# Three reorderings around the V half of a gated decode-attention kernel: idle products and denominators ahead of V's first unit, the last diagonal ahead of a scaling, and w2's extra rows behind O's turning

## The chip, the cores and the metric

The kernel runs on one core of one Trainium2 chip. The metric is the device time of one launch in microseconds. TensorE (PE) does the matrix products, VectorE (DVE) elementwise work, reductions and 32x32 transposes, ScalarE (ACT) exponentials and copies, GpSimd (POOL) builds constants and masks, and SyncE (SP) issues the transfers from device memory. Each engine runs its own list in order; they meet through semaphores.

## What is computed

```python
g = sigmoid((x * gate_w).sum(-1, keepdims=True))
q = x @ wq                      # 2 batches, 32 heads, head size 128, one token
scores = q . k_cache * 128**-0.5   # k_cache, v_cache: (2, 32, 4096, 128) bf16
o = softmax(scores) . v_cache
a = o.reshape(2, 1, 4096) @ wo  # wo: (4096, 512)
b = relu(B_x @ w1) @ w2         # w1: (512, 1376), w2: (1376, 512)
out = g * a + (1 - g) * b
```

One token per batch reads the whole K and V caches, 67 MB each, so there is about one multiply for each byte. (The reference feeds `A_x` to both branches.)

## The kernel before, in words

K and V stream through one SBUF buffer, `kv`, of five regions of 4 MB (A, Ah, B, Bh, C). A K piece is 4 or 8 MB, a V piece ("unit") 8 MB: the eight V units V0 to V7 go by turns into A+Ah (even units) and B+Bh (odd units). SP issues all transfers from one list in order (L339 to L353): the K pieces, the V units, two small transfers of w2's first 96 rows (`w2x`), `wo` in two parts (24 and 8 of its 32 row groups, into region C), and the remaining 1280 rows of w2 in three (`w2b`, `w2c`, `w2d`: 7, 2 and 1 row groups, into Ah). Each waits until the earlier holder of its region has been read: V2 for the last product of V0 (marker `v_read_0`), V3 for that of V1, and so on; the three parts of w2 wait for `v_read_6`.

In the K stage VectorE transposes each quarter of a piece (L483) and TensorE multiplies it with masked queries into four PSUM banks. `softmax` (L527) takes the maximum, lets ScalarE write four exponentials with their sums (`act_exp0` to `act_exp3`), and spreads the weights for V's first unit in two halves (`v_spread`, L552).

In the V stage each unit is 64 products of 32 weights by 512 columns, in four column groups of the array (L582). The unit's sums lie in bank 4 (even) or 5 (odd). `v_loop` is a hardware loop of four rounds, each an even unit, then a run of idle products, then an odd unit. An idle product multiplies constants into a bank that nobody reads; after each even unit there are 1 + `IDLE_ROUNDS` x `IDLE_EACH` = 55 of them. VectorE then takes the "diagonal" of the unit's bank (`v_extract`: a masked multiply, L602, and a reduction, L607).

The end of the kernel is a chain across engines: TensorE gathers the diagonals into O with a selection matrix (`o_gather`), VectorE scales O by the gate and by the reciprocal of the denominators (`o_scale`, once per batch), TensorE turns O into columns (`o_turn`) and VectorE copies them into `oW`. Then `project` multiplies w2's extra rows (indices -4 to -1) and the 32 row groups of `wo`, four at a time, into one bank; VectorE copies that bank (`pr_copy`), and `last_rows` sums it and adds the ten row groups of w2 left (L663, L670, L678). Two copies and one transfer store the 2 KB of output. The order of this end is written out by hand in the last lines of the kernel function; more idle products stand in it (`idle(4)`, `idle(8)`, `idle(4)`). The denominators (`o_denominators`) are two small products on TensorE and two reciprocals on VectorE.

Of the kernel before, what the change touches and what calls it, by code (L numbers as in the profile page):

```python
# [4 lines left out]
ALU = mybir.AluOpType  # L5
ACT = mybir.ActivationFunctionType
AX = mybir.AxisListType
# [10 lines left out]
WO_CUT = 24  # L18
WO_ALL = 32
WIDE = 5  # L20
IDLE_ROUNDS, IDLE_EACH = 6, 9


class _Marker:
# [106 lines left out]
def bass_gated_mix__gqa_block_cached__dense_activation_relu__decode_kernel(  # L131
# [19 lines left out]
    ident16 = sb("ident16", [128, 128], dt.bfloat16)  # L151
# [19 lines left out]
    qbuf = sb("qbuf", [128, 2, 2, 4, 160], dt.bfloat16)  # L171
# [15 lines left out]
    lsum = sb("lsum", [128, 2, 2], dt.float32)  # L187
    sel2 = sb("sel2", [128, WIDE], dt.float32)
    lrow = sb("lrow", [128, 2], dt.float32)
# [18 lines left out]
    def psf(p0, p1, c0, n):  # L208
        return PSF[p0:p1, c0:c0 + n]

    BANK = 512
    V_BANK = (4, 5)
# [11 lines left out]
    IDLE_C0 = 3 * BANK  # L224
# [50 lines left out]
    def dve(fn, waits=(), signal=None, dwaits=()):  # L275
        P.add("dve", fn, waits=[marker(w) for w in waits], signal=marker(signal) if signal else None, dwaits=dwaits)
# [4 lines left out]
    def pe(fn, waits=(), signal=None, dwaits=()):  # L281
        P.add("pe", fn, waits=[marker(w) for w in waits], signal=marker(signal) if signal else None, dwaits=dwaits)
# [5 lines left out]
         waits=["c_i16z"], signal="c_i16")  # L288
# [11 lines left out]
         waits=["c_s1"], signal="c_s2")  # L300
    pool(lambda g: g.affine_select(out=sell_odd, in_=sell_odd, pattern=[[4, 8], [32, 4]],
                                   compare_op=ALU.is_ge, fill=0.0, base=3, channel_multiplier=-1),
         waits=["c_s2"], signal="c_sell")
# [3 lines left out]
         waits=["c_m1"], signal="c_m2")  # L307
# [219 lines left out]
    def softmax():  # L527
        dve(lambda v: v.tensor_reduce(out=mpad[:, 0:2], in_=psf(0, 128, 0, 4 * BANK).rearrange("p (par n) -> p par n", par=2),  # L528
                                      axis=AX.X, op=ALU.max),
            waits=["pe_sc_end", "c_mpad"], signal="dve_m")  # L530
        dve(lambda v: v.transpose(out=mrow[:, :], in_=mpad[:, :]), waits=["dve_m"], signal="dve_mt")
        dve(lambda v: v.tensor_reduce(out=mmax[:], in_=mrow[:, :].rearrange("p (u c) -> p u c", c=4), axis=AX.X, op=ALU.max),
            waits=["dve_mt"], signal="dve_mm")
        dve(lambda v: v.tensor_scalar(out=nrow[:], in0=mmax[:].unsqueeze(2).to_broadcast([128, 8, 4]), scalar1=-INV_SQRT_DH,
                                      scalar2=None, op0=ALU.mult), waits=["dve_mm"], signal="dve_mn")
        dve(lambda v: v.transpose(out=negm[:, :], in_=nrow[:].rearrange("p u c -> p (u c)")),  # L536
            waits=["dve_mn"], signal="dve_neg")
        for g in range(2):
            for par in range(2):
                act(lambda a, g=g, par=par: a.activation(  # L540
                    out=E_sb[:, 32 * g:32 * g + 32, 16 * par:16 * par + 16], in_=psf(0, 128, (2 * par + g) * BANK, 512).rearrange("p (r s) -> p r s", s=16), func=ACT.Exp,
                    bias=negm[:, par:par + 1], scale=INV_SQRT_DH, accum_out=lsum[:, par, g:g + 1]),
                    waits=["dve_neg"], signal=f"act_exp{2 * g + par}")
            dve(lambda v, g=g: v.transpose(out=kt_late[:, 2048 + 1024 * g:3072 + 1024 * g].rearrange("p (r w) -> p r w", w=32), in_=E_sb[:, 32 * g:32 * g + 32, :]),  # L544
                waits=[f"act_exp{2 * g + 1}"], signal=f"dve_et{g}")
            v_spread(0, slice(32 * g, 32 * g + 32))
        dve(lambda v: v.tensor_reduce(out=lrow[:], in_=lsum[:], axis=AX.X, op=ALU.add), waits=["act_exp3"], signal="dve_lrow")  # L547

    def v_weights(n):
        return ptm[:, 2048 * (n % 2):2048 * (n % 2) + 2048].rearrange("p (n h c) -> p n h c", h=8, c=4)  # L550
# [1 line left out]
    def v_spread(n, rows=slice(0, 64), waits=()):  # L552
        shape = [128, rows.stop - rows.start, 8, 4]

        def fn(v):
            ins = v.tensor_tensor(out=v_weights(n)[:, rows], in0=ET_sb[:, rows, 4 * n:4 * n + 4].unsqueeze(2).to_broadcast(shape),  # L556
                                  in1=mask8[:].unsqueeze(1).unsqueeze(3).to_broadcast(shape), op=ALU.mult)
            return ins.then_inc(sem_pt[n % 2], 1) if rows.stop == 64 else ins
        dve(fn, waits=["dve_et1" if rows.stop == 64 else "dve_et0", "c_mask8"] + ([f"v_read_{n - 2}"] if n >= 2 else []))
# [2 lines left out]
        u, halves, region = v_pieces[n]  # L562
        return piece_sb(halves, region).rearrange("p (c n d) -> p c n d", c=4, d=128)

    def idle(n):
        out, lhsT, rhs = psf(0, 32, IDLE_C0, 512), ident16[:, 0:32], qbuf[:, :, :, :, 0:32]
        for j in range(n):
            if j:
                pe(lambda e: mm_held(e, out, lhsT, rhs, True, True, (128, 32), (0, 0)))
            else:  # L570
                pe(lambda e: e.matmul(out, lhsT=lhsT, rhs=rhs, start=True, stop=True, tile_position=(0, 0)))

    def v_loop():
        loop = _Loop(len(v_pieces) // 2)
        P.ops["pe"].append(loop)
        for x in range(2):
            rows = v_moving(x)
            for j in range(64):
                t = j % 4

                def fn(e, j=j, t=t, rows=rows, x=x):
                    ins = e.matmul(psf(32 * t, 32 * t + 32, V_BANK[x] * BANK, 512), lhsT=v_weights(x)[:, j], rhs=rows[:, :, j, :],  # L582
                                   start=(j < 4), stop=(j >= 60), tile_position=(0, 32 * t))
                    take = {0: (sem_pt[x], -1), 1: (sem_v[x], -16), 2: (sem_rd[1 - x], -1), 62: (sem_rd[x], 1)}.get(j)
                    return ins.then_inc(*take) if take else ins
                waits = [(sem_rd[1 - x], 1), (sem_pt[x], 1), (sem_v[x], 16)] if j == 0 else []
                marks = [marker(f"v_read_{2 * m + x}") for m in range(loop.n)] if j == 63 else None
                loop.ops.append(_Step(fn, waits, marks))
            if x == 0:
                out, lhsT, rhs = psf(0, 32, IDLE_C0, 512), ident16[:, 0:32], qbuf[:, :, :, :, 0:32]  # L590
                loop.ops.append(_Step(lambda e: e.matmul(out, lhsT=lhsT, rhs=rhs, start=True, stop=True, tile_position=(0, 0)), [], None))
                inner = _Loop(IDLE_ROUNDS)
                for j in range(IDLE_EACH):
                    inner.ops.append(_Step(lambda e: mm_held(e, out, lhsT, rhs, True, True, (128, 32), (0, 0)), [], None))
                loop.ops.append(inner)
# [14 lines left out]
    def o_denominators():  # L610
        for par in range(2):
            pe(lambda e, par=par: e.matmul(psf(0, 64, L_C0, 1), lhsT=sell[:, 1 - par:65 - par], rhs=lrow[:, par:par + 1],  # L612
                                           start=(par == 0), stop=(par == 1)),
               waits=["dve_lrow", "c_sell", "dve_h2"], signal=("pe_l" if par else None))
        for b in range(2):
            dve(lambda v, b=b: v.reciprocal(out=rinv[:, b:b + 1], in_=psf(32 * b, 32 * b + 32, L_C0, 1)), waits=["pe_l"],
                signal=("dve_rinv" if b else None))

    def o_gather(b, part):
        mine = range(n_first) if b == 0 else range(n_first, len(v_pieces))  # L620
        for n in part:
            w0 = 24 - 8 * (v_pieces[n][0] - 4 * b)
            pe(lambda e, n=n, w0=w0: e.matmul(psf(0, 32, O_C0[b], 128), lhsT=selx[:, w0:w0 + 32], rhs=X2[:, b, n - mine[0], :],  # L623
                                              start=(n == mine[0]), stop=(n == mine[-1])),
               waits=[f"dve_x{n}"] + (["dve_rinv", "dve_selx"] if n == mine[0] else []),
               signal=(f"pe_O{b}" if n == mine[-1] else None))

    def o_scale(b):
        dve(lambda v, b=b: v.tensor_scalar(out=O_sb[:, b, :], in0=psf(0, 32, O_C0[b], 128), scalar1=rinv[:, b:b + 1],  # L629
                                           scalar2=gb[0:32, b:b + 1], op0=ALU.mult, op1=ALU.mult),  # L630
            waits=[f"pe_O{b}", "dve_rinv", "dve_g"], signal=f"dve_O{b}")
# [22 lines left out]
    def pr_copy():  # L654
        dve(lambda v: v.tensor_copy(out=pr_sb, in_=psf(0, 128, PR_C0, 512)), waits=["pe_pr"], signal="dve_pr")
# [48 lines left out]
    softmax()  # L704
    last = len(v_pieces) - 1
    v_spread(1)
    o_denominators()
    v_loop()
    pr_clear()
    for n in range(last):  # L710
# [2 lines left out]
            v_spread(n + 2)  # L713
    o_gather(0, range(n_first))
    o_gather(1, range(n_first, last))
    o_scale(0)
    v_extract(last)
    project(range(-4, 0))
    idle(4)
    o_gather(1, (last,))  # L720
    o_scale(1)
    o_turn()
    idle(8)
    project(range(WO_ALL))
    idle(4)
    pr_copy()
    last_rows()
    store()
# [32 lines left out]
```

## Time and profile before

| what | value |
|---|---|
| time, median of 3 runs (lowest to highest) | 345.71 us (345.55 to 346.44) |
| the profiled execution's own time | 347.16 us |
| its span, first to last instruction | 345.9 us |
| mean granted TensorE clock | 0.887 of full |
| read from device memory | 145.43 MB, 420 GB/s over the span |
| share of the 16 DMA engines in the bulk queue | 97.6% |
| busy: TensorE / VectorE / ScalarE / GpSimd | 241.8 / 186.8 / 9.9 / 14.2 us |

The chain of waits is read from the last instruction back: each line is a start, a length and what ran. "DMA" in it is the time from a transfer's issue to its landing, so it includes waiting behind earlier transfers in the queue. The windows view gives for a stretch of time its length, the busy time of each engine with the count of instructions, the granted TensorE clock (1.00 or 0.50), the DMA share and the rate. A DMA packet of the caches is 64 KB and takes an engine about 2.42 us, and the 16 engines work nearly in step, so in windows of half a microsecond the rate comes in bursts.

### The profile page before, as it was taken

How to read it: one execution, taken by the hardware profiler on the slowest of the kernel's cores; microseconds unless marked ns; L12 is line 12 of the kernel's file. 1: busy time of each engine (PE TensorE's matmuls, PEld its weight loads, DVE VectorE, ACT ScalarE, POOL GpSimd, SP SyncE). 2: the span in 40 equal slices, each digit the busy share in tenths (PEclk: the TensorE clock that was granted, in tenths of full speed). 3: DMA queues.
4: the chain of work that ended last, by engine and by line, in shares of the span. 5: the costliest groups of instructions: out<-in, count | busy, mean ns of one | idle time of the engine just before them, and what ended most of it. 6: DMA issues, size and time to landing. Idle time of an engine off the chain costs nothing.

```text
span 345.9 us, 2803 instructions
## 1 busy us (share of the span) xinstructions
PE 241.8 (70%) x1446; PEld 51.8 (15%) x937; DVE 186.8 (54%) x122; ACT 9.9 (3%) x29; POOL 14.2 (4%) x41
## 2 busy tenths in 40 slices
PE   0467349799789799599899269819940697029797
PEld 0011001111111111011111020202020202011043
DVE  0229079899698999598998574134040040401021
ACT  1050000000000000000000300000000000000000
POOL 6000000000000000000000200000000000000000
PEclk9998959999989999879999859967985699759989
DMA  8998999999899998989999899989899998989892
GB/s 345 424 485 364 485 402 447 424 424 485 364 485 390 442 489 379 470 379 436 451 440 477 379 470 371 464 387 470 387 470 402 455 462 387 470 387 470 383 417 108
DMA packets 3648, 145.49 MB, mean 421 GB/s; under 512 B 413, under 2 KB 548, under 8 KB 828
## 3 DMA queue, kind: packets, MB, share of 16 engines
q1 hardware_dynamic: 3638, 145.43, 97.6%
q8 instruction: 3, 0.05, 0.1%
q10 hardware_dynamic: 6, 0.00, 0.0%
q14 instruction: 1, 0.01, 0.0%
HBM read 145.43 MB, written 0.00 MB: 420 GB/s over the span
## 4 chain that ended last, share of the span: by engine, by line
DMA 60%; DVE 20%; PE 17%; issue 2%; ACT 0%; SPq 0%; DVEq 0%
DMA kv<-in_A_k_cache_dram 32%; DMA kv<-in_A_v_cache_dram 28%; DVE kt L483 17%; PE PS L582 6%; PE PS L489 6%; PE PS L510 2%; DVE kt L556 1%; DVE kt L544 1%; DVE mpad L528 1%; PE PS L650 1%; PE PS L663 0%; ACT kt L540 0%; PE PS L623 0%; DVE kt L607 0%; PE PS L523 0%
## 5 line engine op out<-in xcount | busy, mean ns | idle before, releaser
L483 DVE STREAM_TRANSPOSE kt<-kv 128x2048 f32<-128x2048 f32 x64 | 141.2, 2274 | 25.6 <-DMA kv<-in_A_k_cache_dram 25.6
L510 PE MATMUL PS<-kt,qbuf 128*128 128x512 bf16 x256 | 106.5, 416 | 31.0 <-issue 22.6
L489 PE MATMUL PS<-kt,qbuf 128*128 128x512 bf16 x256 | 106.5, 416 | 0.0
L582 PE MATMUL PS<-kv,kt 128*32 128x512 bf16 x512 | 39.5, 468 | 45.5 <-DMA kv<-in_A_v_cache_dram 45.5
L602 DVE TENSOR_TENSOR kt<-PS,maskc 128x512 f32<-128x512 f32 x8 | 5.5, 688 | 85.6 <-PE PS L582 85.6
L489 PE MATMUL PS<-qbuf,ident 128*32 128x512 bf16 x229 | 50.6, 379 | 0.0
L510 PEld LDWEIGHTS PS<-kt,qbuf 128*128 128x128 bf16 x256 | 25.8, 101 | 140.6 <-issue 140.6
L582 PEld LDWEIGHTS PS<-kv,kt 128*32 128x32 bf16 x512 | 17.1, 114 | 113.0 <-issue 106.0
L556 DVE TENSOR_TENSOR kt<-kt,mask 128x2048 bf16<-128x2048 bf16 (+1 forms) x9 | 18.4, 2046 | 0.1
L407 POOL TENSOR_TENSOR qbuf<-qs,mask 128x64 bf16<-128x64 bf16 x16 | 6.5, 406 | 160.9 <-PE PS L489 141.1
L629 DVE TENSOR_SCALAR O_sb<-PS,rinv,gb 32x128 bf16<-32x128 f32 x2 | 0.8, 398 | 19.2 <-PE PS L623 19.2
L412 PE MATMUL PS<-kv,xTw 128*32 128x320 bf16 (+1 forms) x32 | 5.3, 692 | 5.2 <-DMA kv<-in_A_wq_dram 3.2
L607 DVE TENSOR_REDUCE kt<-kt 128x128 f32<-128x512 f32 x8 | 8.2, 1025 | 0.3
L540 ACT ACTIVATE kt<-PS,negm 128x512 bf16<-128x512 f32 x4 | 2.7, 686 | 168.9 <-DVE negm L536 168.9
L612 PE MATMUL PS<-lrow,sell 128*64 128x1 f32 x4 | 0.6, 250 | 9.8 <-DVE lrow L547 9.8
L436 DVE CAST qrow<-PS 128x256 bf16<-128x256 f32 x2 | 2.6, 1490 | 5.7 <-PE PS L489 5.7
L359 PE MATMUL PS<-ident,x_sb 3*128 3x3 bf16 x4 | 0.3, 167 | 6.7 <-DMA x_sb<-in_gate_w_dram 6.7
L693 ACT ACTIVATE out_sb<-PS 4x128 bf16<-4x128 f32 x1 | 0.3, 268 | 145.9 <-PE PS L678 145.9
L528 DVE TENSOR_REDUCE mpad<-PS 128x2 f32<-128x2048 f32 x1 | 2.3, 2292 | 3.1 <-PE PS L523 3.1
L362 DVE COPY xT<-PS 128x12 bf16<-128x12 bf16 x1 | 0.2, 169 | 7.0 <-PE PS L359 7.0
L489 PE MATMUL PS<-kv,xTw 128*32 128x512 bf16 (+1 forms) x24 | 3.7, 511 | 0.0
L544 DVE STREAM_TRANSPOSE kt<-kt 128x1024 bf16<-128x1024 bf16 x2 | 2.5, 1240 | 1.5 <-ACT kt L540 1.5
(84 smaller groups left out, 47.4 us busy)
## 6 DMA issues: line engine op xcount, KB each, us to landing
kv<-in_A_k_cache_dram SPq DMA_DIRECT2D x4, 4096.0 KB, 30.7
kv<-in_A_wq_dram SPq DMA_DIRECT2D x1, 4096.0 KB, 15.0
kv<-in_A_wo_dram SPq DMA_DIRECT2D x1, 3072.0 KB, 40.1
kv<-in_B_w_dram SPq DMA_DIRECT2D x1, 1376.0 KB, 5.9
kv<-in_A_wo_dram SPq DMA_DIRECT2D x1, 1024.0 KB, 42.2
kv<-in_B_w_dram SPq DMA_DIRECT2D x1, 896.0 KB, 26.1
kv<-in_B_w_dram SPq DMA_DIRECT2D x1, 256.0 KB, 26.4
kv<-in_A_v_cache_dram SPq DMA_DIRECT2D x8, 30.4
```

What stands on the lines that cost most here:

```text
L407: pool(lambda g: g.tensor_tensor(out=out, in0=src, in1=mask, op=ALU.mult).then_inc(sem_q[k % 2], 1), waits=waits)
L412: return e.matmul(out, lhsT=xTw[:, t, :], rhs=rhs, start=(t == 0), stop=(t == 3), tile_position=(0, 32 * c))
L483: dve(lambda v: v.transpose(out=dst, in_=pairs[:, h, 64 * a:64 * a + 64, :]).then_inc(sem_kt[i % SPAN], 1), waits=([f"pe_sc_{i - NKT}"] if ...
L489: return e.add_instruction(mybir.InstMatmult(start_tensor_calc=start, stop_tensor_calc=stop, tile_size=size, tile_position=at, ldweights=F ...
L510: ins = e.matmul(out, lhsT=lhsT, rhs=rhs, start=False, stop=False)
L528: dve(lambda v: v.tensor_reduce(out=mpad[:, 0:2], in_=psf(0, 128, 0, 4 * BANK).rearrange("p (par n) -> p par n", par=2), axis=AX.X, op=ALU ...
L544: dve(lambda v, g=g: v.transpose(out=kt_late[:, 2048 + 1024 * g:3072 + 1024 * g].rearrange("p (r w) -> p r w", w=32), in_=E_sb[:, 32 * g:3 ...
L556: ins = v.tensor_tensor(out=v_weights(n)[:, rows], in0=ET_sb[:, rows, 4 * n:4 * n + 4].unsqueeze(2).to_broadcast(shape), in1=mask8[:].unsq ...
L582: ins = e.matmul(psf(32 * t, 32 * t + 32, V_BANK[x] * BANK, 512), lhsT=v_weights(x)[:, j], rhs=rows[:, :, j, :], start=(j < 4), stop=(j >= ...
L602: dve(lambda e: e.tensor_tensor(out=parts[p0:p1], in0=psf(p0, p1, bank * BANK, 512).rearrange("p (c d) -> p c d", c=4), in1=maskc[p0:p1].u ...
L607: dve(lambda e: e.tensor_reduce(out=X2[:, b, k, :], in_=parts.rearrange("p c d -> p d c"), axis=AX.X, op=ALU.add), waits=[f"dve_m{n}"], si ...
L650: pe(lambda e, t=t, r=r, lhsT=lhsT, rhs=rhs: e.matmul(psf(32 * t, 32 * t + 2, PR_C0, 512), lhsT=lhsT, rhs=rhs, start=(r < 0), stop=(r >= W ...
```

## The change

Four edits. (1) `IDLE_ROUNDS` goes from 6 to 7: 64 idle products after each even unit in place of 55. (2) Before `v_loop`, 9 idle products that wait for the first exponential now stand ahead of the denominators and 5 more behind them, in the bank of the odd units; the sum of the exponentials' sums (`lrow`) moves on VectorE from behind the second half of the spread to behind the first. (3) On VectorE the diagonal of V7 goes ahead of the scaling of O's first batch. (4) On TensorE w2's extra rows move from ahead of the last gather to behind O's turning; the 4 idle products there and the 8 behind the turning go; 4 stand between the 24th and the 25th row group of `wo`, and 3 instead of 4 behind the last one. SP's list of transfers is the same.

```diff
-IDLE_ROUNDS, IDLE_EACH = 6, 9
+IDLE_ROUNDS, IDLE_EACH = 7, 9
...
             v_spread(0, slice(32 * g, 32 * g + 32))
-        dve(lambda v: v.tensor_reduce(out=lrow[:], in_=lsum[:], axis=AX.X, op=ALU.add), waits=["act_exp3"], signal="dve_lrow")
+            if g == 0:
+                dve(lambda v: v.tensor_reduce(out=lrow[:], in_=lsum[:], axis=AX.X, op=ALU.add), waits=["act_exp3"], signal="dve_lrow")
...
-    def idle(n):
-        out, lhsT, rhs = psf(0, 32, IDLE_C0, 512), ident16[:, 0:32], qbuf[:, :, :, :, 0:32]
+    def idle(n, at=IDLE_C0, after=None):
+        out, lhsT, rhs = psf(0, 32, at, 512), ident16[:, 0:32], qbuf[:, :, :, :, 0:32]
...
-                pe(lambda e: e.matmul(out, lhsT=lhsT, rhs=rhs, start=True, stop=True, tile_position=(0, 0)))
+                pe(lambda e: e.matmul(out, lhsT=lhsT, rhs=rhs, start=True, stop=True, tile_position=(0, 0)), waits=[after] if after else [])
...
     v_spread(1)
+    idle(9, V_BANK[1] * BANK, "act_exp0")
     o_denominators()
+    idle(5, V_BANK[1] * BANK)
     v_loop()
...
     o_gather(1, range(n_first, last))
+    v_extract(last)
     o_scale(0)
-    v_extract(last)
-    project(range(-4, 0))
-    idle(4)
     o_gather(1, (last,))
     o_scale(1)
     o_turn()
-    idle(8)
-    project(range(WO_ALL))
+    project(range(-4, WO_CUT))
     idle(4)
+    project(range(WO_CUT, WO_ALL))
+    idle(3)
     pr_copy()
```

## The prediction

> **What bounds the kernel now.** I read the chain of waits first, then the issues, then windows where the chain crosses the change. In the chain, each line is start, length, what ran.
>
> ```profile
> 133.08 29.76 DMA kv<-in_A_k_cache_dram
> ...
> 223.59 27.59 DMA kv<-in_A_v_cache_dram
> ...
> 293.72 34.88 DMA kv<-in_A_v_cache_dram
> 328.60 0.14 issue
> 328.74 5.32 PE PS L582 x64
> 334.06 0.86 PE PS L623 x8
> ...
> 335.35 0.61 DVE kt L602
> ...
> 335.98 1.03 DVE kt L607
> ...
> 338.24 0.32 PE PS L571
> ...
> 342.66 1.56 PE PS L663 x44
> ```
>
> Transfers carry everything up to V7's landing at 293.72 + 34.88 = 328.60; the rest is a tail of 17 us. V3 lands at 223.59 + 27.59 = 251.18, V5 at 289.88 (255.02 + 34.86 in the same chain), so 8 MB take 19.36 us when the queue is full. The K piece of the first line lands at 162.84; from there to V3's landing lie 4 MB of K and four V units, 4.5 x 19.36 = 87.1 us, but 88.34 pass: 1.2 us are lost. The same sum between the K landings at 113.10 and 162.84 (20 MB, 48.4 us, 49.74 taken) loses 1.3 too, so not every loss is a starved queue. Half-microsecond windows (length, busy times of PE, PEld, DVE, ACT, POOL, clock, DMA share, GB/s) show where V's loss is:
>
> ```profile
> 206.50:207.00 0.50, 0.50 (x16) 0.26 (x12) 0.00 (x0) 0.00 (x0) 0.00 (x0) 1.00 3.94 1704
> ...
> 209.00:209.50 0.50, 0.50 (x4) 0.00 (x0) 0.50 (x1) 0.00 (x0) 0.00 (x0) 1.00 2.43 787
> 209.50:210.00 0.50, 0.50 (x4) 0.00 (x0) 0.50 (x2) 0.00 (x0) 0.00 (x0) 1.00 1.11 393
> 210.00:210.50 0.50, 0.50 (x4) 0.00 (x0) 0.50 (x2) 0.00 (x0) 0.00 (x0) 1.00 2.07 786
> ...
> 212.50:213.00 0.50, 0.50 (x5) 0.00 (x0) 0.00 (x0) 0.00 (x0) 0.00 (x0) 1.00 2.72 1180
> ```
>
> Bursts come 2.42 us apart: 206.8, 209.2 and then 211.7 expected. The one at 209 is smeared to 210.5 with a larger share per byte (longer packets), and the next comes at 212.6, about 0.85 late. V2 was issued at 208.27, when V0's last product was read, and V1's transfer ran dry at 209.2. Why V0 was late, and what V7 paid, is in the timeline and in windows:
>
> ```profile
> 202.75 5.44 PE L582 MATMUL PS<-kv,kt 128*32 128x512 bf16 x64
> ...
> 251.32 3.64 PE L582 MATMUL PS<-kv,kt 128*32 128x512 bf16 x64 [1.31 <-DMA kv<-in_A_v_cache_dram]
> ...
> 328.74 5.32 PE L582 MATMUL PS<-kv,kt 128*32 128x512 bf16 x64 [2.47 <-DMA kv<-in_A_v_cache_dram]
> ```
>
> ```profile
> 325.92:329.33 3.41, 0.94 (x14) 0.39 (x16) 0.00 (x0) 0.00 (x0) 0.00 (x0) 1.00 0.96 411
> 329.33:332.74 3.41, 3.41 (x39) 1.57 (x32) 0.00 (x0) 0.00 (x0) 0.00 (x0) 0.50 1.05 454
> ```
>
> The same 64 products take 3.64 at full clock and 5.3 to 5.4 where half of it is granted. V3 (gap 1.31) stayed fast; V7, 2.47 behind the last idle product, met a half-clock stretch of 3.41 us. The end of the queue matters as much:
>
> ```profile
> kv<-in_A_wo_dram SPq DMA_DIRECT2D x1, 1024.0 KB, 42.2
> kv<-in_B_w_dram SPq DMA_DIRECT2D x1, 896.0 KB, 26.1
> kv<-in_B_w_dram SPq DMA_DIRECT2D x1, 128.0 KB, 26.2
> ```
>
> `wo`'s second part, issued at 296.24, lands at 338.4; `w2b`, issued at 314.5, at 340.6; `w2d`, issued at 315.3, at 341.5. TensorE ends at 344.35, so the tail is 2.4 us longer than the transfers allow.
>
> **The change, part by part.** Sums are against the profiled execution, 347.16 us: 1.26 around its span.
>
> *Start of V.* The first exponential is read out at about 196.45. Nine idle products cost 0.427 each at half clock, 0.216 at full (11.82 us for 55 behind V6); they end between 198.4 and 200.3. The `lrow` sum (0.15) comes earlier, at 199.8, so the denominators (0.58) end by 200.9, five more products by 202.0, or 203.0 if all at half clock. V0's weights are ready at 202.2 (0.1 later than before, `lrow` being ahead). So V0 starts at 202.2 to 203.0 against 202.82 and, TensorE having been busy through a 3.4 us stretch, takes 3.7: `v_read_0` at 205.9 to 206.7 against 208.2. V2 is issued at least 1.5 us earlier. Smeared packets began to arrive within 1 to 2 us of the issue at 208.27, so an issue before 207 closes the hole. Value: at most the whole loss, 1.25 (slowest engine, by landings), 0.85 by the bursts, and 0 if the slowest engine's loss has another cause, as the K stage's has. I take 1.05, between the two rows that measure this hole. If V0's cover went (V1's transfer), each microsecond of a later `v_read_0` would cost one.
>
> *64 idle products.* Nine more cost 1.94 us after V0, V2, V4, V6. V1 is waiting then already, but V0 ends 2.3 earlier, so V3 is issued about where it was (223.6), with V2 moving until 229. V3 and V5 start up to 0.7 late; their readers release V5 and V7, which queue 15 us behind other units: nothing. Behind V6 the idle products end at 327.7 (V6 starting 1.05 earlier at half clock, so ending 0.5 earlier) where V7 lands at 327.55 plus 0.14: no gap is left, and V7 takes 3.69 instead of 5.32: 1.63. If V6 runs wholly at half clock (V2 took 6.19), the idle run ends 0.6 later, a price of 0.6 on V7.
>
> *Diagonal ahead of scaling.* Before, VectorE waited for seven gathers (0.86 behind V7's end) and then scaled (0.40) ahead of the diagonal. Now the diagonal (0.61 + 1.03) starts as V7 ends; gathers run beside it; the scaling runs beside the last gather (0.42): 1.29 saved, 0 added.
>
> *The order of the projections.* Turning done, 8 idle products were 1.73 on TensorE's path, of which the copy to `oW` (0.34 and its signals) hid about 0.45: 1.25 saved. The four extra rows (0.22 to 0.4) now run beside that copy. Four idle products between the 24th and 25th row group (0.86) wait in the time in which `wo`'s second part lands; three at the end run beside `pr_copy` (0.69).
>
> Own work of the tail would thus end 1.63 + 1.29 + 1.25 = 4.2 earlier by itself, less up to 0.9 for the inserted idle products: 3.3. It can't all be had: `w2d` lands at 341.5, its products start 0.14 later (as V7's did) and the last ones take 0.3: 341.94 instead of 344.35, so 2.41. With the hole closed all landings come 1.05 earlier, and so does the end (by then the own work is ready: V7 ends at 331.4, `oW` at 334.8, `wo`'s rows done at 338.0, the sums ready at 339.1, `w2b` at 339.55). Sum: 347.16 - 2.41 - 1.05 = **343.7 us**.
>
> The runs shown have a median 1.45 below the profiled execution. Half clock in V7 costs 1.63, so I read this as most runs not paying it (347.16 - 1.63 = 345.53; the lowest is 345.55). The new end hangs on transfers, so 343.7 stands for the runs; if the 1.45 belongs to profiling, it is 342.3.
>
> One page speaks to this. The Trainium skill, "TensorE: Matmul & The Clock Gate", Part 1, says that the clock is granted by a free-running window of 3413 ns; the trace agrees (329.33 to 332.74, 3.41). By that rule the phase differs from run to run, V7's loss is in some runs only, and the gain against the median is about 2.0 rather than 3.5.
>
> **The rivals.** *The hole stays.* V2 waits for something else, or the slowest engine lost its time elsewhere (for: the equal loss in the K stage; against: bursts late just behind V2's issue). Then only the tail is saved: 347.16 - 2.41 = 344.75. The Trainium skill, "DMA: Bandwidth & Descriptors", Specifications, gives about 0.6 us to the first byte for SyncE's transfers; by it V2 could begin at 208.9, before the queue ran dry, and this rival would hold. The smeared packets at 209 to 210.5 speak against it.
>
> *The end goes to half clock.* TensorE now waits in pieces: behind the gathers, around the turning, for `w2b`. The leanest 3.41 us hold about 1.8 busy. In the profile 1.77 busy (288.37 to 291.78) kept full clock, 0.94 lost it. If it is lost, 44 products of 1.56 us take about 1.3 more behind `w2b`, of which 0.2 is hidden: 344.8.
>
> *Slower.* An idle run that overruns: 64 products behind V6 at half clock for two stretches of 3.41 us end 3.4 later, V7 starts at 331.1, and own work (3.69 + 7.7 + 1.4 from V7's start to TensorE's end) ends at 343.9: 346.7. It decides from 2.5 us of overrun. Against it: all four idle runs before were at clock 1.00 throughout.
>
> **How the numbers follow.** Forecast 0.66, with a range of its own of 342.3 to 344.4; hole stays 0.16; half clock at the end 0.12; overrun 0.06. The range of 8 in 10 is 342.3 to 344.9: from the offset case below to both rivals near 344.8. A difference of 0.3%, 1.04 us, is about what can be told from none: 344.67 and 346.75 are the edges. Faster: the forecast and some of the two rivals beside the edge, 0.8; within: most of those two, 0.15; slower: most of the overrun, 0.05.
>
> **What would show it.** V0 starts near 202.3, at 3.6 to 3.8, and SP issues V2 before 207; the bursts keep 2.42 us; V3 lands at 250.2 or less. V7 follows the idle products within 0.3 and takes 3.7. The masked multiply starts with V7's last product. TensorE waits for `w2b` and then `w2d`, and ends within 0.5 of `w2d`'s landing, near 340.9. Wrong would be: V2 issued earlier but landing at 231.8; clock 0.50 behind V7; an idle run that ends over 1 us behind V7's landing.

## The result, and the profile after

The changed kernel takes 343.82 us (median of 10 runs, 343.48 to 345.64), the kernel before in the same runs 346.32 (345.08 to 349.24): a ratio of 0.9933, 95% interval 0.9904 to 0.9961, so 2.3 us less by the ratio and 2.5 by the medians. The forecast was 343.7. The profiled execution of the changed kernel, at 345.64 us, is the slowest of the ten; a second trace of the same kernel (experiment 1) has 343.43. Both are read here, since the difference between them turned out to tell as much as the one between the kernels.

The chain of waits of the changed kernel, first trace (start, length, what):

```profile
202.74 4.46 PE PS L583 x48
207.20 0.02 issue
207.22 25.53 DMA kv<-in_A_v_cache_dram
232.75 0.14 issue
...
315.69 25.78 DMA kv<-in_B_w_dram
341.47 0.04 issue
341.52 1.17 PE PS L664 x36
...
342.84 0.28 DVE out_sb L693
```

The same of the second trace:

```profile
202.27 3.69 PE PS L583 x64
205.96 0.02 issue
205.97 24.49 DMA kv<-in_A_v_cache_dram
230.46 0.14 issue
...
313.63 25.65 DMA kv<-in_B_w_dram
339.27 0.04 issue
339.32 1.17 PE PS L664 x36
```

The end of the chain is no longer V7, gathers, diagonal, scaling and projections. It is the landing of `w2b`, the first and largest of w2's last three parts, and behind it 36 products. The prediction, too, had w2's transfers as the bound, but by way of the last part, `w2d`. The timeline shows the new order of the tail (second trace: start, busy time, engine, line, operation; in brackets the idle time before and what ended it):

```profile
327.36 3.64 PE L583 MATMUL PS<-kv,kt 128*32 128x512 bf16 x64
330.81 1.69 PE L624 MATMUL PS<-kt,selx 128*32 128x128 f32 x14
331.07 0.69 DVE L603 TENSOR_TENSOR kt<-PS,maskc 128x512 f32<-128x512 f32 x1 [15.68 <-PE PS L583]
331.79 1.03 DVE L608 TENSOR_REDUCE kt<-kt 128x128 f32<-128x512 f32 x1
...
334.72 1.47 PE L651 MATMUL PS<-kv,oW 128*2 128x512 bf16 x24 [0.34 <-DMA kv<-in_A_wo_dram]
...
339.32 1.17 PE L664 MATMUL PS<-kv,hT 128*4 128x128 bf16 x36 [0.19 <-DMA kv<-in_B_w_dram]
340.32 0.22 PE L489 MATMUL PS<-kv,hT 128*32 128x128 bf16 x2
```

The diagonal starts as V7's last product ends, beside the gathers. TensorE waits for `wo` and then for `w2b`. The last line shown is the first product of `w2d`'s row: it follows the 36 without a wait. V7 takes 3.64, right behind the idle products. From V7's landing to TensorE's last product 13.27 and 13.38 us pass in the two traces, 15.73 before; by the prediction's sum it was to be 13.34.

What differs between the two traces is the front. V0 took 4.62 in the first and 3.64 in the second, and V2 was issued at 207.22 and 205.97. The table has this for all traces of the study; landings are read from the signals that each of the 16 DMA engines gives for its share, so that the typical engine (median) can be told from the slowest, for which every reader has to wait. "End" is the end of TensorE's last product, and "w2" in the last column is the landing of `w2d`. V0's time runs from its first product to its last; in experiment 8 idle products run among V0's, so that it takes 4.69 there at full clock.

```
trace                     V0 takes  V2 issued  V2 lands: typical, slowest  V7 lands  end behind V7  end behind w2
before                        5.44     208.27     229.91    231.83           328.60       15.73          2.79
changed, first                4.62     207.22     229.09    232.75           329.53       13.27          0.33
1  changed, second            3.64     205.97     229.12    230.46           327.22       13.38          0.38
9  changed, third             3.64     205.91     229.03    230.56           327.32       13.38          0.35
2  start alone                3.64     206.04     228.99    230.50           327.25       14.04          1.09
3  64 idle products alone     6.15     208.92     230.46    233.36           330.55       14.75          1.83
4  both edits of the tail     6.22     208.77     230.26    231.86           328.64       13.30          0.34
5  changed, old start         6.55     209.22     230.75    232.38           329.16       13.30          0.36
6  changed, 55 products       3.79     206.21     229.12    230.83           327.58       14.24          1.28
7  a quarter of w2            3.64     206.18     229.19    231.04           327.82       13.04          2.20
8  V0 held back               4.69     209.41     230.94    232.56           329.34       13.31          0.38
10 warm start                 3.64     206.09     229.17    230.57           327.32       13.30          0.34
11 diagonal alone             5.58     208.25     229.87    232.48           329.25       13.44          0.52
12 projections alone          5.27     207.89     230.22    232.61           329.44       13.66          0.75
```

In the changed kernel's second trace V7 lands 1.38 us earlier than in the trace before (the prediction: 1.05), and the tail behind it is 2.35 shorter (2.41).

### The profile page after: what moved, and what is told of

The parts are those of the page before. It is cut to its first block, busy times and chain, and to the rows that moved or that the text cites. A ratio compares the mean times of both kernels' runs of the same rounds, so it can differ in the third digit from the quotient of the medians.

```text
span 344.4 us, 2854 instructions
## 1 busy us (share of the span) xinstructions
PE 251.2 (73%) x1487; PEld 52.1 (15%) x938; DVE 187.0 (54%) x122; ACT 9.9 (3%) x29; POOL 14.2 (4%) x41
## 4 chain that ended last, share of the span: by engine, by line
DMA 65%; DVE 19%; PE 13%; issue 2%; ACT 0%; SPq 0%; DVEq 0%
DMA kv<-in_A_k_cache_dram 32%; DMA kv<-in_A_v_cache_dram 26%; DVE kt L483 17%; DMA kv<-in_B_w_dram 7%; PE PS L583 6%; PE PS L489 3%; PE PS L510 2%; DVE mpad L528 1%; ACT kt L540 0%; DVE kt L544 0%; DVE kt L557 0%; PE PS L664 0%; PE PS L523 0%; PE PS L613 0%; PE PS L572 0%
## 5 line engine op out<-in xcount | busy, mean ns | idle before, releaser
L489 PE MATMUL PS<-kt,qbuf 128*128 128x512 bf16 x256 | 106.5, 416 | 0.0
L583 PE MATMUL PS<-kv,kt 128*32 128x512 bf16 x512 | 38.7, 452 | 39.3 <-DMA kv<-in_A_v_cache_dram 39.3
L489 PE MATMUL PS<-qbuf,ident 128*32 128x512 bf16 x269 | 61.2, 387 | 0.0
L572 PE MATMUL PS<-qbuf,ident 128*32 128x512 bf16 x4 | 1.8, 438 | 4.1 <-ACT kt L540 4.1
L489 PE MATMUL PS<-kv,xTw 128*32 128x512 bf16 (+1 forms) x24 | 3.5, 468 | 0.0
L439 PE MATMUL PS<-ident,qrow 128*128 128x128 bf16 x8 | 1.0, 311 | 2.7 <-DVE qrow L436 2.7
```

The costliest lines, as they stand in the source:

```text
L489: return e.add_instruction(mybir.InstMatmult(start_tensor_calc=start, stop_tensor_calc=stop, tile_size=size, tile_position=at, ldweights=F ...
```

## The experiments

The theory: every landing up to w2's moves with the moment at which V2 is issued, since the queue is full at all other times, and the tail's own work hardly shows once it is below w2's landing. The rivals: the slowest DMA engine did not starve, so the start gives nothing; or the tail's own work still sets the end. Ratios are to the kernel before, with their 95% intervals; 1 to 4, 5 to 8 and 9 to 12 shared a chip and its runs of before (medians 345.90, 345.99, 346.37). A median of experiments 5 to 12 set beside experiment 1's is thus one from another group of runs, so the ratio is given where the two say different things.

### 1. The changed kernel, a second trace

> The changed kernel itself, as a yardstick on the chip that the three parts run on, and a second trace of it. My theory: the end is set by the landing of w2's last part, so TensorE ends 0.3 to 0.5 us behind that landing, about 13.3 us behind V7's landing (15.75 before), whatever the clock's phase; 2.0 to 2.7 us faster than before. Rival (the tail's own work sets the end): no wait for w2 in the chain, and the distance from V7's landing to TensorE's end differs from the 13.29 of the first trace by more than 0.5.

Measured: 343.45 (343.38 to 343.68), 0.9934 (0.9914 to 0.9953). TensorE ends 0.38 behind w2's landing, 13.38 behind V7's, though the first trace had other clock phases and landed V7 2.3 later. In both traces TensorE starts 0.04 behind `w2b`'s landing and does not pause again. The end hangs on the transfer.

### 2. The start of V alone

```diff
+            if g == 0:
+                dve(lambda v: v.tensor_reduce(out=lrow[:], ...
...
+    idle(9, V_BANK[1] * BANK, "act_exp0")
     o_denominators()
+    idle(5, V_BANK[1] * BANK)
     v_loop()
```

> Edit 2 alone: idle products and denominators ahead of V0, 6 idle rounds and the old tail. My theory: V2 is issued 1 to 2.3 us earlier, V1's transfer no longer runs dry, and all later landings come earlier: 0.85 to 1.05 us faster. Rival (the slowest of the 16 DMA engines sets each landing and did not starve): the typical engine gains, the slowest doesn't, and the time is that of before within 0.3 us.

Measured: 344.25 (344.10 to 346.00), 0.9961 (0.9941 to 0.9981): by the ratio 1.35 us, by the medians 1.65. The slowest engine gains too: V2 lands at 230.50. The rival falls. The expected 0.85 to 1.05 lies within the interval (0.7 to 2.0) but below both figures. One reason is in the table: the trace from which it was sized issued V2 at 208.27, and the other traces with the old start do so between 207.89 and 209.22, three of the five later than 208.7. With V7 at full clock the old tail ends 14.04 behind V7; the 15.73 of before less the 1.68 that V7 lost there (5.32 against 3.64) is 14.05.

### 3. The 64 idle products alone

```diff
-IDLE_ROUNDS, IDLE_EACH = 6, 9
+IDLE_ROUNDS, IDLE_EACH = 7, 9
```

> 64 idle products instead of 55, alone. My theory: V7 always runs at full clock and TensorE ends about 14.1 us behind V7's landing instead of 15.75 where before met half clock there, so 0.7 to 0.9 us faster in the median if half the runs of before met it, 1.6 if all did. Rival (the clock's phase saved most runs already, or the end hides it): within 0.3 us of before.

Measured: 345.93 (345.44 to 348.22), 0.9998 (0.9985 to 1.0010). My figure of 0.7 to 0.9 falls and the rival holds: in the median the longer idle run is worth nothing. What it does is seen in single executions. In the trace of this kernel V6 took 6.45, at half clock almost throughout, the idle run ended late, and V7 took 4.32.

### 4. Both edits of the tail alone

```diff
     o_gather(1, range(n_first, last))
+    v_extract(last)
     o_scale(0)
-    v_extract(last)
-    project(range(-4, 0))
-    idle(4)
...
-    idle(8)
-    project(range(WO_ALL))
+    project(range(-4, WO_CUT))
     idle(4)
+    project(range(WO_CUT, WO_ALL))
+    idle(3)
```

> Edits 3 and 4 alone: the diagonal ahead of the scaling and the new order of the projections, with 6 idle rounds and the old start of V. My theory: where V7 runs at full clock the end comes down to w2's landing, 0.75 us; where it meets half clock the own work of the tail decides and 1.1 us are saved: 0.7 to 1.2 us faster. Rival (own work all the way): 1.29 + 1.25 less 0.86 for the inserted idle products, 1.7 us faster.

Measured: 344.84 (344.58 to 345.28), 0.9975 (0.9962 to 0.9987): 0.87 by the ratio, 1.06 by the medians, where own work would have given 1.7. The chain of waits of this kernel has the cover in it, with everything ahead of w2 as in the kernel before:

```profile
315.15 25.46 DMA kv<-in_B_w_dram
340.61 0.04 issue
340.65 1.17 PE PS L663 x36
```

### 5. The changed kernel with the old start

```diff
-    idle(9, V_BANK[1] * BANK, "act_exp0")
     o_denominators()
-    idle(5, V_BANK[1] * BANK)
```

(and `lrow` back at its old place)

> The changed kernel without edit 2: V0 starts at half clock with nothing ahead of it. My theory: V2 is issued when V1's transfer has run dry, the typical engine lands V2 at 229.9 to 230.5 instead of 229.1, and the end moves by as much as edit 2 alone gained: 1.0 to 1.5 us slower than the changed kernel (344.5 to 345.0). Rival (edits 2 and 3 to 4 pay from the same wait at the end, so one covers the other): 0 to 0.4 us slower.

Measured: 345.06 (344.10 to 345.37), 0.9955 (0.9931 to 0.9979). The median is 1.6 above experiment 1's, but by the ratios it is 0.7 us, with intervals that overlap, so the times alone do not part theory and rival. The traces do: V7 lands 1.94 later than in experiment 1, and the end lies as far behind w2 (0.36 against 0.38). The start does not pay from the wait at the end. Its chain of waits shows the late V0 and the late V2:

```profile
202.66 6.54 PE PS L582 x49
209.20 0.02 issue
209.22 23.16 DMA kv<-in_A_v_cache_dram
232.38 0.14 issue
```

### 6. The changed kernel with 55 idle products

```diff
-IDLE_ROUNDS, IDLE_EACH = 7, 9
+IDLE_ROUNDS, IDLE_EACH = 6, 9
```

> The changed kernel with 55 idle products instead of 64. My theory: V7 meets half clock in the runs whose window falls badly and ends 1.6 us later there, but with the shorter tail some 1.2 us of it hide behind w2's landing: 0 to 0.2 us slower in the median, up to 0.6 in single runs. Rival (the ninth-to-64th products carry the gain that the prediction gave them): 0.7 us or more slower in the median.

Measured: 343.64 (343.38 to 344.67), 0.9928 (0.9906 to 0.9950): 0.2 above experiment 1 by the medians, no difference by the ratios, as expected; the rival's 0.7 does not show. The traced execution met the half clock in V7 (5.32 us); its windows, with length, busy times and, third from the end, the clock:

```profile
324.90:328.31 3.41, 0.94 (x14) 0.39 (x16) 0.00 (x0) 0.00 (x0) 0.00 (x0) 1.00 0.95 404
328.31:331.72 3.41, 3.41 (x40) 1.57 (x32) 0.00 (x0) 0.00 (x0) 0.00 (x0) 0.50 0.97 418
```

TensorE ended 14.24 behind V7 there instead of 13.38: of the 1.68 that V7 loses, 0.86 reaches the end and the rest hides behind w2.

### 7. A quarter of w2's transfers

```diff
-e.dma_start(w2[:, r0:r1, :], w2_in[:, r0:r1, :])
+e.dma_start(w2[:, r0:r1, 0:128], w2_in[:, r0:r1, 0:128])
```

> The changed kernel with w2b, w2c and w2d loading 128 of their 512 columns; the other columns of these rows are left out, so the output is not the reference's. 0.98 MB less, so w2's last part would land some 2.2 us earlier. My theory: w2's landing sets the end, but the next bound is close behind it: wo's second part lands 3.1 us ahead of w2d, and eight products, the copy, the sums and w2's products take 2.9 us from there, so 0.4 to 0.7 us faster than the changed kernel. Rival (own work sets the end): no faster.

Measured: 343.38 (343.16 to 343.70), 0.9918 (0.9889 to 0.9947): 0.07 below experiment 1 by the medians, 0.6 by the ratios, with intervals that overlap. The trace says how much of the expected 0.4 to 0.7 can be had: TensorE now ends 2.20 behind w2 and 13.04 behind V7, so 0.34 earlier relative to V7, and the chain of waits names what took over:

```profile
295.55 42.14 DMA kv<-in_A_wo_dram
337.69 0.04 issue
337.73 0.63 PE PS L651 x8
338.36 0.02 issue
338.39 0.70 DVE kt L656
339.09 0.04 issue
339.13 1.61 PE PS L664 x44
```

The landing of `wo`'s second part and 3.17 us of work behind it (2.9 had been assumed) are a bound 0.3 us ahead of that of w2. Two transfers bound the end nearly alike; own work ahead of both has room (`wo`'s first part is waited for as well).

### 8. V0 held back

```diff
-    idle(5, V_BANK[1] * BANK)
+    idle(21, V_BANK[1] * BANK)
     v_loop()
```

> The changed kernel with 21 idle products instead of 5 behind the denominators, so that V0 starts about 3 us late at full clock. My theory: an issue of V2 behind 207.2 opens the hole behind V1 again: V2 is issued at about 209, its typical landing moves from 229.1 to 230.8, and the end by 1.6 to 2.0 us. Rival (V2's issue had slack; edit 2 gains at another place): within 0.3 us of the changed kernel.

Measured: 345.57 (344.61 to 346.58), 0.9983 (0.9963 to 1.0003): 2.1 above experiment 1 by the medians, 1.7 by the ratios, and the rival falls. The only thing done is to let V0 end late. The windows show the hole that this opens in the queue (GB/s in the last column):

```profile
206.50:207.00 0.50, 0.50 (x16) 0.20 (x8) 0.00 (x0) 0.00 (x0) 0.00 (x0) 1.00 3.03 1311
...
209.00:209.50 0.50, 0.50 (x4) 0.04 (x1) 0.09 (x1) 0.00 (x0) 0.00 (x0) 1.00 0.01 0
209.50:210.00 0.50, 0.50 (x4) 0.00 (x0) 0.50 (x1) 0.00 (x0) 0.00 (x0) 1.00 0.00 0
210.00:210.50 0.50, 0.50 (x4) 0.00 (x0) 0.47 (x2) 0.00 (x0) 0.00 (x0) 1.00 2.80 918
210.50:211.00 0.50, 0.50 (x4) 0.00 (x0) 0.50 (x1) 0.00 (x0) 0.00 (x0) 1.00 3.48 1180
```

Bursts at 206.5 and, instead of at 209, at 210.0 to 211.0. The same stretch of experiment 1 has its burst in place:

```profile
206.50:207.00 0.50, 0.50 (x4) 0.00 (x0) 0.47 (x2) 0.00 (x0) 0.00 (x0) 1.00 3.33 1442
...
209.00:209.50 0.50, 0.50 (x4) 0.00 (x0) 0.50 (x1) 0.00 (x0) 0.00 (x0) 1.00 2.79 1180
```

### 9. The changed kernel once more

> The changed kernel once more, beside the next three on the same chip, and a third trace of it. My theory: most runs at 343.4 to 343.9; a part of them 1 to 2 us longer where the idle products of the start run at half clock for two windows, V0 ends behind 207 and one DMA engine waits for V2's descriptors.

Measured: 343.59 (343.42 to 344.68), 0.9930 (0.9905 to 0.9955); two of six runs above 344.1. Over all 22 runs of this kernel five are above 344.1 and the rest lie between 343.38 and 343.95.

### 10. A warm start

```diff
-    idle(9, V_BANK[1] * BANK, "act_exp0")
+    idle(34, V_BANK[1] * BANK)
     o_denominators()
-    idle(5, V_BANK[1] * BANK)
+    idle(7, V_BANK[1] * BANK)
```

> The changed kernel with 34 idle products that follow K's last product at once instead of 9 that wait for the first exponential, and 7 instead of 5 behind the denominators. My theory: the clock never falls, V0 takes 3.6 to 3.7 us from 202.2 to 202.5 in every run, V2 is issued at 205.9 to 206.2, and the long runs of the changed kernel go: the median 0 to 0.3 us faster than the changed kernel, the highest run within 0.6 us of the lowest. Rival (the long runs come from where code fetches fall, not from V0): same spread as the changed kernel, same median.

Measured: 343.47 (343.30 to 343.50), 0.9917 (0.9895 to 0.9940). The six runs lie within 0.2 us, the highest below the median of the changed kernel beside it. Its timeline shows no gap behind K's last products (L523), and V0 at full clock as soon as its weights are ready:

```profile
191.36 1.02 PE L523 MATMUL PS<-qbuf,ident 128*128 128x512 bf16 x4
...
192.54 7.29 PE L489 MATMUL PS<-qbuf,ident 128*32 128x512 bf16 x33
...
202.39 3.64 PE L583 MATMUL PS<-kv,kt 128*32 128x512 bf16 x64 [0.60 <-DVE kt L557]
```

This is the best version of the study, by 0.1 us in the median and by its lack of long runs. Six runs without a long one are not proof where five of 22 were long; the trace has the mechanism.

### 11. The diagonal alone

```diff
     o_gather(1, range(n_first, last))
+    v_extract(last)
     o_scale(0)
-    v_extract(last)
```

> Edit 3 alone in the kernel before: V7's diagonal ahead of the scaling of O's first batch. My theory: 1.29 us less of own work, of which 0.7 to 0.8 shows before w2's landing sets the end where V7 runs at full clock, and all of it where it doesn't: 0.7 to 1.2 us faster, TensorE ending 13.3 to 13.5 behind V7's landing. Rival (the eight idle products behind the turning hide the copy chain, so that the earlier diagonal only moves the idle time): under 0.4 us faster.

Measured: 345.55 (344.56 to 347.47), 0.9982 (0.9964 to 1.0001): 0.6 by the ratio, 0.8 by the medians, an interval that just touches no change. In the trace the old tail with the early diagonal ends 13.44 behind V7, against 14.04 in experiment 2, both with V7 at 3.64: 0.60 saved, and w2's landing reached but for 0.2. The trace speaks against the rival; the runs alone, with this interval, do not exclude its "under 0.4". Why 0.60 and not 1.29 is in the chain of waits:

```profile
329.38 3.64 PE PS L582 x64
333.02 1.29 PE PS L623 x12
...
334.95 0.65 PE PS L489 x3
335.60 0.23 PE PS L623 x2
335.83 0.03 issue
335.86 0.41 DVE O_sb L629
```

The diagonal is not in it: it ends at 334.86, but the last gather (L623 x2) starts only behind w2's extra rows and the idle products (L489), which stand ahead of it in the old order. Edit 4 takes them away. The gain sized for edit 3 needs edit 4.

### 12. The order of the projections alone

```diff
-    project(range(-4, 0))
-    idle(4)
     o_gather(1, (last,))
...
-    idle(8)
-    project(range(WO_ALL))
+    project(range(-4, WO_CUT))
     idle(4)
+    project(range(WO_CUT, WO_ALL))
+    idle(3)
```

> Edit 4 alone in the kernel before: w2's extra rows behind the turning, four idle products between the row groups, three at the end. My theory: 1.25 us less behind the turning, 0.86 us more between the row groups: 0.3 to 0.5 us faster. Rival (the inserted idle products fall in the wait for wo's second part and cost nothing): 0.7 us or more faster.

Measured: 346.94 (345.83 to 349.56), 1.0020 (0.9998 to 1.0042): no gain, if anything a loss, against 0.3 to 0.5 expected. The trace, an execution near the low end of its runs, has the 0.38 (13.66 behind V7 against 14.04). What the other runs lost is not shown by it. One reading, argued only: with the old order on VectorE and the idle products gone, TensorE is lean behind V7. Its windows (first busy time: TensorE's):

```profile
333.20:336.60 3.40, 1.91 (x19) 1.38 (x14) 2.02 (x3) 0.00 (x0) 0.00 (x0) 1.00 0.92 393
```

The like stretch behind V7 has 2.51 us in the changed kernel's second trace (331.00 to 334.40) and 2.91 in experiment 11's (333.00 to 336.40). The leanest 3.41 us are leaner still: 1.31 here (334.45 to 337.86), 2.20 in the changed kernel's second trace (331.35 to 334.76). By the prediction's own rows 1.77 kept the clock and 0.94 lost it, so a run whose clock window falls there could lose the clock in the tail, the prediction's rival of a half clock at the end. No trace of this kernel caught it, and it stays open.

## Why the prediction was right, and where it was not

**The bound at the end** held in its size, and the wait inside it was the wrong one. "`w2d` lands at 341.5, its products start 0.14 later and the last ones take 0.3" was to leave 2.41 of the tail's saving; 2.46 and 2.35 were measured from V7's landing in the two traces. But no trace has a wait at `w2d`. Where w2 sets the end (the three traces of the changed kernel, experiments 4, 5 and 8), the first product of `w2b` starts 0.04 behind its landing, 40 products follow without a pause in 1.28 us, and `w2d`, 0.94 to 1.00 behind `w2b`, has landed 0.05 to 0.11 before its row's turn comes. With the landing of `w2b` in the trace before, 340.56, that gives 341.88, where the prediction had 341.94 by way of `w2d`. That the two ways agree is luck.

Experiment 4 shows the cover from the other side: the tail's edits alone give 0.9 to 1.1 where own work would have given 1.7. The diagonal, sized at 1.29 for itself, shows 0.60 alone, because the extra rows and idle products ahead of the last gather then set the pace (experiment 11). With both edits the last gather starts 1.88 behind V7's end in the second trace instead of 3.00, so 1.12 are saved there. In every trace with both edits of the tail, all of w2's transfers and V7 near full clock, TensorE ends 0.33 to 0.38 behind w2. How near the next bounds lie was not in the prediction: `w2d` at most 0.1 us, `wo`'s second part 0.3 us (experiment 7).

**The hole behind V1** held as a mechanism, and its size was the term that was off. 1.05 was taken; alone it measured 1.35 by the ratio (interval 0.7 to 2.0), and V7 lands 1.38 earlier. The sizing used one execution, in which V0 took 5.44. In the table the 1.38 has two parts. The typical engine lands V2 0.79 earlier (229.91 to 229.12), close to the 0.85 "by the bursts". The rest is that the slowest engine lies 1.92 behind the typical one before and 1.34 now, and most of that comes from a code fetch. Now and then one DMA engine carries 16 KB of the program's own instructions, and one such fetch falls into V2's transfer in every trace (at 222.74 before, 221.34 in the second trace). Followed from packet to packet, the engine that made it is the one that lands V2 last in eleven of the 14 traces, in three of these level with another. Before, it lands 0.61 behind the next engine, in the second trace 0.05. So the hole itself was sized well for the typical engine, and up to 0.6 of what looked like its value is where a fetch fell.

The same answers the prediction's doubt about the K stage, "loses 1.3 too". There a fetch comes at 116.08: from the K landing at 113.10 to the next, 4 MB, the typical engine takes 9.76 us and the slowest 11.02. In the first trace of the changed kernel the fetch comes at 56.87; there the slowest engine takes 20.82 for the 8 MB from 45.27 on instead of 19.36, and nothing is lost from 114.52 to 124.22 (4 MB, 9.70). The rival "the hole stays" is excluded as a whole by experiments 2, 5 and 8; its "the slowest engine lost its time elsewhere" is true of a part.

**The clock of V7** is where the reasoning was half wrong. The sum counted 1.63 for it within the profiled execution, and the text allowed that most runs do not pay it. Alone the 64 products bring nothing in the median (experiment 3), and removing them costs 0.2 by the medians and nothing by the ratios (experiment 6). The stretch that explained the difference between the profiled execution and the median was only one of two: runs of before range over more than 4 us, as V0's half-clock time (5.27 to 6.55 in the traces) moves the landings as well. That the forecast of 343.7 stood for the runs all the same is in part because the new end hangs on transfers, and in part luck. The second trace is 347.16 - 2.35 - 1.38 = 343.43, the first 347.16 - 2.46 + 0.93 = 345.63, and most runs lie near the former. And against the runs of before the gain is 2.3 to 2.5 and not the "about 2.0" of the prediction, since ten runs of before have a median of 346.32 where the first three had 345.71.

The Trainium skill's sentence on the free-running window of 3413 ns ("TensorE: Matmul & The Clock Gate", Part 1) is borne out: in the traces the half-clock stretches of the V stage are whole multiples of 3.41 us (3.4, 6.8, 10.2 and more), and in three traces of one kernel V0 took 4.62, 3.64 and 3.64.

**"An issue before 207 closes the hole"** was nearly right, and the step before it failed: "TensorE having been busy through a 3.4 us stretch", V0 was to take 3.7. In the first trace of the changed kernel it took 4.62:

```profile
197.70:201.11 3.41, 3.16 (x11) 0.60 (x5) 3.34 (x5) 0.89 (x4) 0.00 (x0) 0.50 0.75 327
201.11:204.52 3.41, 3.41 (x24) 0.96 (x24) 3.41 (x3) 0.00 (x0) 0.00 (x0) 0.50 1.33 577
204.52:207.20 2.68, 2.68 (x50) 1.27 (x41) 0.65 (x3) 0.00 (x0) 0.00 (x0) 1.00 0.96 416
```

A stretch that the row calls busy for 3.16 of 3.41 did not raise the clock; the 2.94 of 195.88 to 199.29 in the second trace did. Likewise 3.04 (201.71 to 205.12 in experiment 5) did not, and 2.64 and 2.72 in experiments 7 and 9 (195.82 to 199.23, 195.59 to 199.00) did. The denominators stand in the two that did not (four passes of a single column, 0.59 us): without them these hold 2.57 and 2.45. The three that did have none in them. That the denominators do not count towards the clock is argued from these five stretches, not shown by a run that moves them alone. So V2 went out at 207.22, and for one engine that was too late. In the packets' records 15 engines go on without a gap or with a short one, and one packet of V2 starts at 210.55 and takes 3.43 us instead of 2.42: that engine is 2.1 us behind its fellows. At 221.23 a code fetch of 16 KB takes 0.96 us at the moment when a packet of this late sequence ends, and the next one takes 2.89. The records carry no engine's name; they are joined by starts that follow ends within 5 ns. Together it is 3.5 us: V2's slowest engine lands 3.66 behind the typical one, 1.34 in experiment 1, and that difference of 2.3 is in every later landing and in the time (345.64 against 343.43). The prediction's own sign of being wrong, V2 issued earlier but landing at 231.8, was met in this execution (207.22 and 232.75): V7 lands 0.93 later than before, and all that it gains comes from the tail.

**The half clock at the end** and **the overrun** were seen in no trace of the changed kernel: behind V7 the clock is 1.00 until TensorE is done, and the leanest 3.41 us hold 2.20 us of work in the second trace where the prediction had 1.8. In experiment 10's trace V6 ran at half clock almost throughout (6.30), V7's products run among the last idle ones and take 4.20, and the end does not move: 13.30 behind V7's landing.

## What to carry to other kernels

Where a queue of transfers is full, look for the one place where it runs dry, and read who issues the next transfer there: 64 products at half clock, on no bound of their own, cost over a microsecond through a late issue. Ahead of work that you shorten at the end, add up the landings of the last transfers first; they say how much of the saving can show, and a second and a third may lie 0.1 and 0.3 us ahead of the last one. A clock that follows the engine's own activity makes one profiled execution a sample of many: size such a term from several traces, and prefer a version that never lets the clock fall (experiment 10) to one that usually recovers in time.

## What was not expected of the hardware

A transfer issued into a dry queue does not start on all engines at once. In experiment 8 the first packet of V2 starts 0.95 us behind the issue and the last engine's 1.42; in experiments 5 and 3 it is 0.95 for the first, and 1.8 and 3.5 for the last, and the first packets take 2.6 to 3.7 us instead of 2.42. The Trainium skill gives about 0.6 us to the first byte ("DMA: Bandwidth & Descriptors", Specifications); the measured start of the first packet, 0.95, is later, and the issue has to be early enough for the last engine, up to 3.5 us. And a code fetch of 16 KB, three in each trace, costs one engine of a full queue 1.4 us that it never makes up: 0.96 or so for itself, and 2.88 or 2.89 instead of 2.42 for the engine's next packet, in V2's transfer in all 14 traces. In the first trace of the changed kernel it struck the engine that was already late, and the slowest engine stays 3.7 behind the typical one from V2's landing to V7's.
